# A 13-row store on one core, cut into blocks of 112, 12 and 4 partitions

## The chip, the cores and the metric

The kernel runs on one core of a Trainium2 chip. The metric is the device time of the whole program in microseconds (us). A core has five instruction streams: TensorE (PE), VectorE (DVE), ScalarE (ACT), GpSimd (POOL) and SyncE (SP). SP computes nothing; here it issues the transfers between the chip's main memory (DRAM) and the core's own memory, in which a tile has 128 partitions. The transfers are carried out by the core's 16 DMA engines.

## The reference

The input x has shape (1, 384, 384, 384) in bf16, channels last; w1d has a single element. Each channel's mean over all 384 x 384 positions is multiplied by that element, a sigmoid makes a scale per channel of it, and x is multiplied by the scale:

```python
g = jnp.einsum("bhwc->bc", x) / (H * W)
...
s = _sigmoid(g * w1d[0])     # k = 1, so there is no neighbour to add
return x * s[:, None, None, :]
```

(The third line is written out for k = 1.) The scale isn't known before all of x has been read, and x is 113 MB, more than the core's memory holds. A part of x has to be read twice.

## The kernel before

**Layout.** The 147456 positions are 1152 rows of 128 partitions; one row is 384 channels, 768 bytes in each partition. One tile named `arena` takes nearly the whole core memory and is addressed by rows. The input is cut into two chunks. `STREAMED` are rows that are read in the first pass, summed and dropped, and read again in the second pass. `KEPT` are rows that stay in the core between the passes. In each chunk partition p holds a contiguous stretch of DRAM, so that a transfer of n rows is 128 pieces of n x 768 contiguous bytes, one per partition.

**First pass.** Loads (`load`, line 235) bring rows in; TensorE sums them into PSUM (`sum_rows`, line 246). Many of the kept rows are packed so that four rows take three (`fold`, on VectorE and ScalarE); others are kept raw. At the end ScalarE computes the sigmoid (line 433) and copies it to PSUM (line 437).

**Second pass.** VectorE and GpSimd multiply rows by the scale (`scale`, line 446), packed rows are first unfolded (`unfold`, lines 280 and 286), and `store` (line 465) writes rows to the output. Rows that have been stored come free, and further rows of `STREAMED` are loaded into them, multiplied and stored. The raw kept rows go first, in ten pieces from `landed` (line 650 on) and three more that GpSimd multiplies (`alongside`); the last of the ten is `(A, 13)`, the 13 rows from row `A` of the arena on. Their place inside `KEPT` is `raw(A)`.

**Order.** All large transfers are issued by SP, in the order in which a planner (the loop from line 719 on) writes them out. The planner simulates time in steps of 0.05 us with costs per row and per transfer, and decides when a store or a load joins the list. The first load of the second pass is allowed only once all raw pieces have been sent. `Flow` (line 21) records every step and derives the waits: a step that overwrites arena rows waits for each step that reads them, and the transfers of one engine go round 24 semaphores (`LANES`), so that one of them also waits for the one 24 places earlier.

For the profile, the end of the first pass is at 267 us. After that SP issues 14 stores from 268.34 us on, with the changed one the last of them, at 280.67. Then follow three loads: 21 rows at 281.18, 13 rows, and at 287.77 13 rows into the place of the rows that the changed store reads. The next stores come from 295.25 on.

Of the kernel before, what the change touches and what calls it, by code (L numbers as in the profile page):

```python
# [131 lines left out]
def kernel(  # L132
# [11 lines left out]
    nc = tc.nc  # L144
    P = nc.NUM_PARTITIONS
# [18 lines left out]
    A = V + PAIR  # L164
# [27 lines left out]
    arena = pool.tile([P, ROWS, C], bf16, name="arena")  # L192
# [11 lines left out]
    of = out.rearrange("b h w c -> (b h w) c")  # L204

    def view(t, r0, n):
        return t[r0 * P : (r0 + n) * P, :].rearrange("(p r) c -> p r c", r=n)

    def rows(lo, n):
        return [("a", r) for r in range(lo, lo + n)]  # L210

    fl = Flow(nc, tc)
# [5 lines left out]
    STREAMED, KEPT = (0, N_STREAM + 1), (N_STREAM + 1, N_KEPT - 1)  # L218
# [9 lines left out]
    def raw(a):  # L228

        return c_raw + 1 + (a - U if a < G0 else PAIR + a - V)  # L230
# [65 lines left out]
    def fold(k):  # L296
# [46 lines left out]
        reads=["ones", "w_bf"], writes=["bank0"],  # L343
# [4 lines left out]
        reads=["bank0"], writes=["w_sc"],  # L348
# [38 lines left out]
    for i, bk in enumerate(banks):  # L387
        lo, hi = i * BANK, min((i + 1) * BANK, PS * C)
# [36 lines left out]
    for a, n in [(U, 8), (A, 20), (A + 20, 11), (A + 31, 8), (V, 8), (Y + 1, 6), (T + 5, 4), (T + 2, 3), (T, 2)]:  # L425
# [8 lines left out]
        reads=["bank0", "w_sc"], writes=["s_bf"],  # L434
# [6 lines left out]
    def scale(a, n, eng="DVE", s=s_bf, after=()):  # L441
        v = arena[:, a : a + n, :]
        vec = nc.vector if eng == "DVE" else nc.gpsimd
        fl.add(
            eng,
            lambda: vec.tensor_tensor(  # L446
                out=v, in0=v, in1=s[:, None, :].to_broadcast([P, n, C]), op=Op.mult
            ),
            reads=rows(a, n) + ["s_bf" if s is s_bf else "bank0"], writes=rows(a, n), after=after,
        )  # L450
# [6 lines left out]
    def scale_both(a, n):  # L457
# [4 lines left out]
        if m:  # L462
            scale(a + n - m, m, "POOL", after=before)

    def store(chunk, a, lo, hi):
        r0, n = chunk
        return fl.add(
            "SP",
            lambda: nc.sync.dma_start(out=view(of, r0, n)[:, lo:hi, :], in_=arena[:, a : a + hi - lo, :]),  # L469
            reads=rows(a, hi - lo), dma=True,  # L470
        )

    def unfold(g, first):

# [244 lines left out]
    while True:  # L719
# [12 lines left out]
        if dve_at <= now:  # L732
# [4 lines left out]
            if landed and (ahead < PENDING or not can):  # L737
                chunk, a, lo, n, end = landed.popleft()
# [18 lines left out]
        if alongside and alongside[0][0] <= now:  # L757
            _, chunk, a, lo, n = alongside.popleft()
            store(chunk, a, lo, lo + n)
            moves.append([now + LAT, n * ROW + PER_STORE, stored(a, n)])  # L760
        while waiting and waiting[0][0] <= now:
            _, n, then, chunk, a, lo, known = waiting.popleft()
            known.append(store(chunk, a, lo, lo + n))
            last_is_load = False
            sent_off += 1
            moves.append([now + LAT, n * ROW + PER_STORE, then])
# [10 lines left out]
        if bank_at is None and len(line) <= total - BANKS_AT and got and max(got)[0] > PS * 4 // 3:  # L777
            a = max(got)[1]
# [3 lines left out]
            for i, bk in enumerate(banks):  # L782
                lo, hi = i * BANK, min((i + 1) * BANK, PS * C)
# [6 lines left out]
        if got and todo < N_STREAM:  # L790
            n, a = max(got)
            n = min(n, CAP, N_STREAM - todo)
# [62 lines left out]
```

## Time and profile before

| | |
|---|---|
| median of three runs | 719.0 us (718.45 to 719.02) |
| the profiled execution | 718.35 us, its span 716.0 us |
| moved by DMA | 303.68 MB, 424 GB/s over the span |
| read from and written to DRAM | 190.32 MB and 113.25 MB |
| large transfers issued by SP | 110 |
| mean granted TensorE clock | 0.668 |

The span goes from the first to the last instruction; what lies around it belongs to the time but not to the profile. The profile lists busy time by engine, the chain of waits that ended last, and transfers with their size in KB (1024 bytes) and the time from issue to landing. A window is a stretch of the span with the busy time of every engine, the share of the 16 DMA engines that was busy, and GB/s; a packet (one contiguous piece of a transfer) is counted in the window in which it starts, so that short windows are coarse.

### The profile page before, as it was taken

How to read it: one execution, taken by the hardware profiler on the slowest of the kernel's cores; microseconds unless marked ns; L12 is line 12 of the kernel's file. 1: busy time of each engine (PE TensorE's matmuls, PEld its weight loads, DVE VectorE, ACT ScalarE, POOL GpSimd, SP SyncE). 2: the span in 40 equal slices, each digit the busy share in tenths (PEclk: the TensorE clock that was granted, in tenths of full speed). 3: DMA queues.
4: the chain of work that ended last, by engine and by line, in shares of the span. 5: the costliest groups of instructions: out<-in, count | busy, mean ns of one | idle time of the engine just before them, and what ended most of it. 6: DMA issues, size and time to landing. Idle time of an engine off the chain costs nothing.

```text
span 716.0 us, 2027 instructions
## 1 busy us (share of the span) xinstructions
PE 211.7 (30%) x1202; PEld 0.3 (0%) x3; DVE 467.5 (65%) x383; ACT 116.5 (16%) x97; POOL 98.1 (14%) x46
## 2 busy tenths in 40 slices
PE   4667967999598680000000000000000000000000
PEld 0000000000000000000000000000000000000000
DVE  4600001799989849999999999999940597006840
ACT  3700001476667630000110000000000000000000
POOL 0000000000000005414233431167100000000000
PEclk9899998999899995555555555555555555555555
DMA  9999999999999989999999999999999999999997
GB/s 375 434 446 419 439 431 425 452 417 434 427 430 426 429 349 384 412 414 435 425 430 436 441 425 436 457 421 421 455 409 458 426 425 445 430 428 436 442 438 308
DMA packets 15852, 303.68 MB, mean 424 GB/s; under 512 B 1762, under 2 KB 2274, under 8 KB 4962
## 3 DMA queue, kind: packets, MB, share of 16 engines
q1 hardware_dynamic: 15840, 303.57, 99.0%
q8 instruction: 4, 0.07, 0.0%
q14 instruction: 6, 0.05, 0.0%
q10 hardware_dynamic: 2, 0.00, 0.0%
HBM read 190.32 MB, written 113.25 MB: 424 GB/s over the span
## 4 chain that ended last, share of the span: by engine, by line
DMA 48%; DVE 29%; PE 16%; ACT 1%; issue 1%; DVEq 0%; another core or an unknown queue 0%; SPq 0%; POOLq 0%
DMA arena<-in_x_dram 37%; DVE arena L446 20%; PE bank L246 16%; DMA out_dram<-arena 12%; DVE arena L280 5%; DVE arena L286 4%; ACT arena L317 1%; DVEq L107 0%; SPq L240 0%; SPq L469 0%; ACT s_bf L433 0%; SPq L113 0%; SPq L850 0%; POOLq L107 0%
## 5 line engine op out<-in xcount | busy, mean ns | idle before, releaser
L246 PE MATMUL bank<-arena,ones 128*128 128x384 bf16 x1151 | 203.6, 341 | 46.6 <-DMA arena<-in_x_dram 46.6
L280 DVE TENSOR_SCALAR arena<-arena 128x1536 uint16<-128x1536 uint16 (+2 forms) x199 | 140.4, 750 | 105.2 <-DMA arena<-in_x_dram 98.3
L446 POOL TENSOR_TENSOR arena<-arena,s_bf 128x768 bf16<-128x768 bf16 (+3 forms) x42 | 97.9, 2334 | 426.8 <-ACT bank L437 267.9
L446 DVE TENSOR_TENSOR arena<-arena,bank 128x3072 bf16<-128x3072 bf16 (+13 forms) x61 | 138.0, 2303 | 4.8 <-DMA arena<-in_x_dram 4.1
L446 DVE TENSOR_TENSOR arena<-arena,s_bf 128x5376 bf16<-128x5376 bf16 (+4 forms) x27 | 76.5, 2901 | 94.9 <-DMA arena<-in_x_dram 84.8
L286 DVE TENSOR_TENSOR arena<-arena 128x3072 uint16<-128x3072 uint16 (+2 forms) x90 | 117.6, 1307 | 13.9 <-PE bank L246 11.1
L317 ACT ACTIVATE arena<-arena 128x3072 uint16<-128x3072 uint16 (+1 forms) x38 | 102.4, 2696 | 146.0 <-DVE arena L280 146.0
L556 PE MATMUL bank<-odd,ones 128*128 128x1 bf16 x1 | 0.2, 187 | 260.0 <-DVE odd L551 260.0
L384 ACT COPY arena<-bank 128x512 uint32<-128x512 uint32 (+2 forms) x8 | 4.2, 534 | 88.0 <-DMA out_dram<-arena 87.8
L246 PE MATMUL bank<-s_bf,ones 128*128 128x384 bf16 x48 | 8.3, 326 | 0.0
L317 ACT ACTIVATION_READ_ACCUMULATOR arena<-arena 128x1 f32 x38 | 7.1, 186 | 0.0
L384 ACT COPY bank<-arena 128x512 uint32<-128x512 uint32 (+2 forms) x8 | 3.8, 529 | 0.0
L260 PE MATMUL bank<-arena,ones 128*128 128x384 bf16 x1 | 0.5, 477 | 7.0 <-DMA arena<-in_x_dram 7.0
L433 ACT ACTIVATE s_bf<-bank,w_sc 128x384 bf16<-128x384 f32 x1 | 0.6, 581 | 9.4 <-PE bank L246 9.4
L823 ACT ACT_TABLE_LOAD x1 | 1.3, 1283 | 0.7 <-PEq L839 0.7
L337 DVE MEMSET ones<- 128x128 bf16 x1 | 0.2, 165 | 1.0 <-PEq L839 1.0
L342 PE MATMUL bank<-w_bf,ones 1*128 1x1 bf16 x1 | 0.2, 178 | 2.1 <-DMA w_bf<-in_w1d_dram 2.1
L347 DVE TENSOR_SCALAR w_sc<-bank 128x1 f32<-128x1 f32 x1 | 0.2, 158 | 0.9 <-PE bank L342 0.9
L560 DVE CAST odd_i<-bank 128x1 int32<-128x1 f32 x1 | 0.2, 157 | 0.3 <-PE bank L556 0.3
L437 ACT COPY bank<-s_bf 128x192 uint32<-128x192 uint32 x1 | 0.3, 323 | 0.0
L556 PEld LDWEIGHTS bank<-odd,ones 128*128 128x128 bf16 x1 | 0.1, 105 | 517.9 <-DVE odd L551 517.9
L384 ACT COPY arena<-rest 128x64 uint32<-128x64 uint32 x1 | 0.2, 246 | 0.0
(10 smaller groups left out, 1.4 us busy)
## 6 DMA issues: line engine op xcount, KB each, us to landing
arena<-in_x_dram SPq DMA_DIRECT2D x3, 6912.0 KB, 36.2
out_dram<-arena SPq DMA_DIRECT2D x3, 6912.0 KB, 28.4
arena<-in_x_dram SPq DMA_DIRECT2D x4, 4608.0 KB, 24.2
arena<-in_x_dram SPq DMA_DIRECT2D x6, 3072.0 KB, 19.4
out_dram<-arena SPq DMA_DIRECT2D x6, 3072.0 KB, 21.5
arena<-in_x_dram SPq DMA_DIRECT2D x2, 6144.0 KB, 31.4
arena<-in_x_dram SPq DMA_DIRECT2D x2, 4992.0 KB, 23.1
arena<-in_x_dram SPq DMA_DIRECT2D x1, 8160.0 KB, 26.4
```

What stands on the lines that cost most here:

```text
L246: return pe.add_instruction(mybir.InstMatmult(name=nc.get_next_instruction_name(), ins=[pe.lower_ap(rhs), pe.lower_ap(ones[:])], outs=[pe. ...
L260: return nc.tensor.matmul(acc, lhsT=ones[:], rhs=arena[:, i, :], start=first, stop=last)
L280: lambda: nc.vector.tensor_scalar(out=dst, in0=src, scalar1=s0, scalar2=s1, op0=op0, op1=op1),
L286: "DVE", lambda: nc.vector.tensor_tensor(out=dst, in0=a, in1=b, op=op), reads=reads, writes=writes
L317: lambda: nc.scalar.activation(out=y, in_=y, func=ACTF.Copy, accum_out=seen[:, 2 * k + i : 2 * k + i + 1]),
L337: fl.add("DVE", lambda: nc.vector.memset(ones[:], 1.0), writes=["ones"])
L384: "ACT", lambda: nc.scalar.copy(dst.bitcast(u32), src.bitcast(u32)), reads=reads, writes=writes
L433: lambda: nc.scalar.activation(out=s_bf[:], in_=acc, func=ACTF.Sigmoid, scale=w_sc[:, 0:1]),
L437: "ACT", lambda: nc.scalar.copy(s_ps.bitcast(u32), s_bf[:].bitcast(u32)), reads=["s_bf"], writes=["bank0"]
L446: lambda: vec.tensor_tensor(out=v, in0=v, in1=s[:, None, :].to_broadcast([P, n, C]), op=Op.mult),
L556: lambda: nc.tensor.matmul(votes, lhsT=ones[:], rhs=odd[:], start=True, stop=True),
L823: nc.scalar.preload_act_table(ACTF.Sigmoid)
```

## The change

The store whose chunk is `KEPT` and whose first row is `raw(A)`, the 13 rows from arena row `A`, is issued as three transfers, of partitions 0 to 111, 112 to 123 and 124 to 127. All other stores are issued as before. The planner still counts one store, and `store` returns the last of the three steps. A step that later overwrites these rows waits for all three.

```diff
+    STEPPED = raw(A)
+    BLOCKS = (0, 112, 124, P)
+
     def store(chunk, a, lo, hi):
         r0, n = chunk
-        return fl.add(
-            "SP",
-            lambda: nc.sync.dma_start(out=view(of, r0, n)[:, lo:hi, :], in_=arena[:, a : a + hi - lo, :]),
-            reads=rows(a, hi - lo), dma=True,
-        )
+        cuts = BLOCKS if (chunk, lo) == (KEPT, STEPPED) else (0, P)
+        for p, e in zip(cuts, cuts[1:]):
+            step = fl.add(
+                "SP",
+                lambda p=p, e=e: nc.sync.dma_start(
+                    out=view(of, r0, n)[p:e, lo:hi, :], in_=arena[p:e, a : a + hi - lo, :]
+                ),
+                reads=rows(a, hi - lo), dma=True,
+            )
+        return step
```

## Prediction

> **What bounds the kernel now.** I read the page first, for the part that is full, and then the windows of busy time by stretch, which carry bytes per second.
>
> ```profile
> span 716.0 us, 2027 instructions
> PE 211.7 (30%) x1202; PEld 0.3 (0%) x3; DVE 467.5 (65%) x383; ACT 116.5 (16%) x97; POOL 98.1 (14%) x46
> ...
> DMA  9999999999999989999999999999999999999997
> ...
> q1 hardware_dynamic: 15840, 303.57, 99.0%
> ```
>
> No compute engine is busy for two thirds of the span, while the 16 DMA engines are 99.0% busy on the one queue that SP issues. The time is set by bytes over DMA rate, and by whatever makes a DMA engine move bytes below its rate. So I looked for stretches in which the queue is full and the rate sags. The last two columns are the DMA share and GB/s.
>
> ```profile
> core 0: us, PE busy (x) PEld busy (x) DVE busy (x) ACT busy (x) POOL busy (x), PEclk, DMA share, GB/s
> 266.50:269.00 2.50, 0.80 (x5) 0.00 (x0) 1.05 (x3) 0.90 (x2) 0.65 (x1) 1.00 0.00 0
> ...
> 271.00:277.00 6.00, 0.00 (x0) 0.00 (x0) 6.00 (x4) 0.00 (x0) 6.00 (x3) 0.50 1.04 419
> 277.00:281.00 4.00, 0.00 (x0) 0.00 (x0) 4.00 (x4) 0.00 (x0) 0.56 (x1) 0.50 1.02 426
> ...
> 285.00:288.00 3.00, 0.00 (x0) 0.00 (x0) 2.90 (x4) 0.00 (x0) 0.00 (x0) 0.50 1.04 319
> 288.00:296.00 8.00, 0.00 (x0) 0.00 (x0) 6.79 (x4) 0.00 (x0) 2.38 (x2) 0.50 0.98 417
> 296.00:299.00 3.00, 0.00 (x0) 0.00 (x0) 3.00 (x2) 0.00 (x0) 2.53 (x2) 0.50 1.01 395
> 299.00:314.00 15.00, 0.00 (x0) 0.00 (x0) 14.86 (x10) 0.00 (x0) 4.74 (x2) 0.50 1.02 433
> 314.00:318.00 4.00, 0.00 (x0) 0.00 (x0) 3.93 (x3) 0.00 (x0) 0.00 (x0) 0.50 0.96 349
> ...
> 330.00:708.00 378.00, 0.19 (x1) 0.10 (x1) 268.77 (x154) 4.41 (x9) 71.17 (x31) 0.50 1.01 434
> ```
>
> From 330 to 708 us the rate is 434 GB/s without a break, across many switches between loads and stores. Between 285 and 318 us it sags three times although the engines count as busy (share 0.96 to 1.04), so packets take longer there; no engine lacks work. Against 434 the sags cost (434-319)x3/434 = 0.8 us, (434-395)x3/434 = 0.3 us and (434-349)x4/434 = 0.8 us, together 1.9 us for the mean DMA engine. The first sag begins where the store of the change meets the first load of the second pass:
>
> ```profile
> 280.67 0.33 SPq L469
> ...
> 281.18 12.22 DMA arena<-in_x_dram
> ```
>
> These are two pieces of the chain of waits: the store issued at 280.67 and the load at 281.18. The DMA view gives the time from issue to landing: of the 13-row store before it, of the changed store, and of the first and the third load of the second pass:
>
> ```profile
> out_dram<-arena SPq DMA_DIRECT2D x1, 1248.0 KB, 4.9
> ...
> out_dram<-arena SPq DMA_DIRECT2D x1, 1248.0 KB, 7.1
> ...
> arena<-in_x_dram SPq DMA_DIRECT2D x1, 2016.0 KB, 12.2
> ...
> arena<-in_x_dram SPq DMA_DIRECT2D x1, 1248.0 KB, 12.6
> ```
>
> The changed store lands at 280.67 + 7.1 = 287.8, having waited for what was queued ahead. The other end of the program shows how the DMA engines stand to each other (the last three stores on the timeline, the last one's time to landing, then the windows):
>
> ```profile
> 664.64 24.36 SPq L469 DMA_DIRECT2D out_dram<-arena  x3
> ...
> out_dram<-arena SPq DMA_DIRECT2D x1, 6816.0 KB, 25.9
> ...
> 709.40:710.60 1.20, 0.00 (x0) 0.00 (x0) 0.00 (x0) 0.00 (x0) 0.00 (x0) 0.50 0.94 409
> 710.60:711.50 0.90, 0.00 (x0) 0.00 (x0) 0.00 (x0) 0.00 (x0) 0.00 (x0) 0.50 0.01 0
> 711.50:712.60 1.10, 0.00 (x0) 0.00 (x0) 0.00 (x0) 0.00 (x0) 0.00 (x0) 0.50 0.35 149
> ```
>
> The last issue ends at 664.64 + 24.36 = 689.0 and takes 0.33, so it began near 688.66. A window counts a packet where it starts. The last store is 71 rows, so a packet is 71 x 768 = 54.5 KB: 149 x 1.1 = 164 KB are three packets. Three engines thus begin their last packet after 711.5, when all others have begun theirs before 710.6. The three run 0.9 us behind at the least; between the middles of the two groups (710.0 and 712.05) it is 2.0 us, which I take. The span ends with those three: the other thirteen have about 2.0 us of slack.
>
> **The change, part by part.** The bytes stay. One row of the store is 13 x 384 x 2 B = 9984 B per partition; an engine moves 426/16 = 26.6 GB/s (277 to 281 us), so a packet of one partition takes 0.375 us, and the whole store 8 packets per engine, 3.0 us.
>
> The 112 block is 7 packets for each of 16 engines. The 12 block can be at most one packet on 12 engines and the 4 block one packet on 4, if a partition is not cut. If both start from the same engine, four engines carry 9, eight carry 8 and four carry 7. The engines then reach the load up to two packets apart, 0.75 us. [...] No run here shows the assignment yet.
>
> Price of the extra packet: +0.375 us for the engines with 9, nothing for those with 8, -0.375 for those with 7. This is the lower bound, since a packet cannot beat its engine. The upper bound: the full store moves all 128 partitions in 3.0 us, so if it is the partitions (or what stands in front of a few of them) that limit and not the engines, a block takes 3.0 us however narrow; an engine with both small blocks then spends 7 x 0.375 + 3.0 + 3.0 = 8.6 us in place of 3.0, +5.6. I take the lower end, +0.4, for the forecast, since the tail's packets go with a single engine's rate: three alone show no other pace than all (a 54.5 KB packet at 26.6 GB/s is 2.05 us, and 712.6 + 2.05 = 714.65 is just the landing of the last store, 688.66 + 25.9 = 714.56). Those are big packets of whole stores, so I keep both ends for the range.
>
> [...]
>
> Issue: two more DMAs on SP at the 0.33 us of the row above put the first load from 281.18 to about 281.85. The cover is the stores queued ahead, which keep the engines busy until the changed store lands at 287.8, so it costs nothing; uncovered it would be 0.7 us. Completion of two more transfers: 271 to 277 us, with stores of 3 to 7 rows, runs at 419 against 434, 0.2 us in 6 us over some seven transfers: 0.03 each, 0.06 in all.
>
> The wait that follows: the third transfer of the second pass overwrites these 13 rows, so it now waits for three stores, and its SP instruction holds back what is queued behind.
>
> ```profile
> 281.18 6.91 SPq L240 DMA_DIRECT2D arena<-in_x_dram  x3
> ...
> 293.42 12.21 DVE L446 TENSOR_TENSOR arena<-arena,bank 128x3072 bf16<-128x3072 bf16 x5 [1.21 <-DMA arena<-in_x_dram]
> ...
> 295.25 8.54 SPq L469 DMA_DIRECT2D out_dram<-arena  x4
> ```
>
> Behind it stand the stores from 295.25, which wait for VectorE's multiplies of the first load, landed at 293.4. At 287.8 the two loads ahead still hold 3264 KB, 7.7 us of work; the wait can come 5 us later before an engine runs dry. Cost nothing, up to +5 us of lateness. The semaphore lanes shift by two, but the transfer 24 back is tens of microseconds old.
>
> What may go: the sags. After the first pass the DMA engines stand still (266.5 to 269 us, share 0.00) and start together, so 16 us later all switch from writing HBM to reading it in step, and the rate drops to 319. Once they have drifted apart, no switch sags. If the step keeps them from switching together, the first sag of 0.8 us goes for all, and the lag of the three, which can only have been made where engines are slowed unequally, is not built up, or less. The most to be had is 0.8 + 2.0 + 0.8 (the 314 sag) - 0.4 = 3.2 us, rounded up by the 296 sag to 3.5; the least that I call this case is 1.4. I take the three's 2.0, plus the first sag's 0.8, less 0.4 of extra packet, less 0.3 for what stays of the lag: -2.1 us. The profiled execution took 718.35 us, 2.35 around the span of 716.0; it becomes 716.25, with a span of 713.9. The median of the runs is 719.0, 0.65 above the profiled one, so 716.9.
>
> **Rivals.**
> *Nothing that a measurement of this kernel can tell (within 0.2%, 1.44 us).* The sags belong to what is read and written there, not to the step: then packets move by -0.4 to +0.4 us and the result is 718.6 to 719.4. For it: the sag at 314 to 318 comes 45 us after the common start, when engines are no longer together. Against it: no sag after 330 with the same kinds of switches. Here too belongs a first sag that goes alone, 0.8 - 0.4 = 0.4 us faster with the lag kept.
>
> *Slower: the narrow blocks crawl.* Place: the 12 and the 4 block. Price: between +0.4 and +5.6 us on the engines that carry both; the middle is 3.0. It decides where those engines have no cover: in the thirteen, 2.0 us is hidden, and it takes over 2.0 + 1.44 = 3.4 us to be slower by 0.2%; if they are among the three, or become late ones for which the later sags work as for the three now, 1.44 us does. [...] For it: late engines seem to be the ones that grow later. Against it: the packets of the three at the end keep the pace of one engine.
>
> *That the split doesn't happen* I give nothing: the condition asks for the chunk and the row of the 13 at A, which alone begin there, and each tail piece is sent by itself.
>
> **How the numbers follow.** Engines out of step, sags and lag mostly gone: 0.46, 715.3 to 717.56 us, likeliest 716.9; its own range with a weaker effect 715.3 to 717.9. No difference that can be told: 0.23, about 719. Slower by the narrow blocks: 0.31, 720.44 to over 722. The range that leaves out 2 in 10 runs from 715.3 (719.0 - 3.5, rounded) to 721.6, and loses the far end of the slow case (about 0.13) and a little below.
>
> **What would show it.** Right: the windows 285 to 288 and 314 to 318 above 380 GB/s in place of 319 and 349, and at the end no gap in packet starts as that from 710.6 to 711.5. Slower: the last of the three small stores lands over 3 us after the 112 block, and more than three packets start late at the end. No difference: the windows within 20 GB/s of before and three late packets. Wrong altogether if the span changes while the GB/s from 285 to 318 and the tail do not, or if SP or VectorE, not DMA, begins to hold the queue dry after 288 us.

## The result, and the profile after

The changed kernel is slower: 721.2 us against 719.0 us in the same session, ratio 1.0039 with a 95% interval of 1.0027 to 1.0052 (2.8 us, 1.9 to 3.7). Faster by 2.1 us was forecast; the value lies inside the stated range, on the other side of no change, and only because the range had been drawn wide enough for the slower rival. Where a ratio and a difference of medians disagree, here and below, the ratio with its interval is the one used.

The page after, its first lines and its DMA packets:

```profile
span 718.8 us, 2030 instructions
...
DMA packets 15868, 303.68 MB, mean 422 GB/s; under 512 B 1778, under 2 KB 2290, under 8 KB 4978
```

The bytes are the same. The page of before has 15852 packets, 1762 of them under 512 B. SP's queue had 15840 packets before, which are 110 large transfers with 128 + 16 each: one for each partition and 16 small ones, as many as there are DMA engines. I read the small ones as one for each engine that a transfer uses; the 16 new ones are then 12 + 4. The completion events in the trace of after agree: 16 for the 112 block, 12 for the 12 block and 4 for the 4 block, beside one at the issue of each of the small two. By this reading the small blocks used 12 and 4 engines; neither count tells which engines they are.

The windows of after at the stretches that the prediction read (last columns: DMA share and GB/s):

```profile
271.00:277.00 6.00, 0.00 (x0) 0.00 (x0) 6.00 (x4) 0.00 (x0) 6.00 (x3) 0.50 1.04 418
277.00:281.00 4.00, 0.00 (x0) 0.00 (x0) 4.00 (x4) 0.00 (x0) 0.63 (x1) 0.50 1.03 431
281.00:285.00 4.00, 0.00 (x0) 0.00 (x0) 3.93 (x4) 0.00 (x0) 0.00 (x0) 0.50 1.03 386
285.00:288.00 3.00, 0.00 (x0) 0.00 (x0) 2.93 (x3) 0.00 (x0) 0.00 (x0) 0.50 0.96 286
288.00:296.00 8.00, 0.00 (x0) 0.00 (x0) 4.25 (x3) 0.00 (x0) 0.00 (x0) 0.50 0.98 373
...
299.00:314.00 15.00, 0.00 (x0) 0.00 (x0) 14.93 (x9) 0.00 (x0) 6.93 (x4) 0.50 1.00 410
314.00:318.00 4.00, 0.00 (x0) 0.00 (x0) 3.90 (x4) 0.00 (x0) 0.00 (x0) 0.50 1.09 376
318.00:322.00 4.00, 0.00 (x0) 0.00 (x0) 3.96 (x3) 0.00 (x0) 0.00 (x0) 0.50 0.90 360
330.00:708.00 378.00, 0.19 (x1) 0.10 (x1) 271.11 (x155) 4.40 (x9) 72.79 (x32) 0.50 1.01 434
```

Up to 281 us and from 330 us on, the rates are those of before. In between lies most of the loss. One window over it, before and then after:

```profile
281.00:322.00 41.00, 0.00 (x0) 0.00 (x0) 39.41 (x24) 0.00 (x0) 11.64 (x6) 0.50 1.01 409
```

```profile
281.00:322.00 41.00, 0.00 (x0) 0.00 (x0) 36.82 (x23) 0.00 (x0) 9.65 (x5) 0.50 0.99 384
```

Against 434 GB/s that is (434 - 409) x 41/434 = 2.4 us lost before and (434 - 384) x 41/434 = 4.7 us after: 2.3 us more, of the 2.8 us by which the two spans differ. The rate falls by 6 per cent and the DMA share by 2 (1.01 to 0.99), so most of it is packets that take longer, and the smaller part engines without work. The chain of waits of after shows what else moved:

```profile
280.74 0.35 SPq L474
...
281.12 1.28 SPq L474
...
282.44 1.40 SPq L474
...
284.03 12.03 DMA arena<-in_x_dram
```

SP issues the 112 block in 0.35 us, the 12 block in 1.28 and the 4 block in 1.40, so that the first load is issued at 284.03 in place of 281.18. It lands at 296.06 in place of 293.40.

### The profile page after: what moved, and what is told of

It is laid out like the page before. It is cut to its first block, busy times and chain, and to the rows that moved or that the text cites. A ratio compares the mean times of both kernels' runs of the same rounds, so it can differ in the third digit from the quotient of the medians.

```text
span 718.8 us, 2030 instructions
## 1 busy us (share of the span) xinstructions
PE 213.1 (30%) x1202; PEld 0.3 (0%) x3; DVE 467.4 (65%) x383; ACT 116.5 (16%) x97; POOL 98.0 (14%) x46
## 4 chain that ended last, share of the span: by engine, by line
DMA 48%; DVE 29%; PE 16%; ACT 1%; SPq 1%; issue 1%; DVEq 0%; another core or an unknown queue 0%; POOLq 0%
DMA arena<-in_x_dram 37%; DVE arena L446 20%; PE bank L246 16%; DMA out_dram<-arena 11%; DVE arena L280 5%; DVE arena L286 4%; ACT arena L317 1%; SPq L474 0%; DVEq L107 0%; SPq L240 0%; ACT s_bf L433 0%; SPq L113 0%; SPq L858 0%; POOLq L107 0%
```

## The experiments

Three theories: **width** (transfers of fewer than 128 partitions move below the engines' rate), **step** (engines with 9, 8 and 7 packets reach the load unevenly), **queue** (SP's queue holds few transfers, so that two more of them delay the first load). Each kernel was timed beside the kernel before, in the same session. The edits below are abridged.

**At the place of the change.** The store cut by rows in place of partitions (rows3), the uncut store with a delayed first load (late), the cut made in an earlier store (earlier), and blocks of 112 and 16 (b112_16):

```diff
 rows3     BLOCKS = (0, 5, 9, 13), and out=view(of, r0, n)[:, lo + p : lo + e, :]
 earlier   STEPPED = raw(A + 13)
 b112_16   BLOCKS = (0, 112, P)
 late      store as before;
+          for i in range(22): hold = [fl.add("ACT", copy one column of a small tile, reads=rows(A, 1))]
-          load(STREAMED, a, todo, todo + n)
+          load(STREAMED, a, todo, todo + n, after=hold)      # first load of the second pass alone
```

> The 13-row store is cut by rows instead of partitions: 5, 4 and 4 rows of all 128 partitions. As many transfers as in the changed kernel, none narrow, all engines even. If SP's short queue is the cause (every transfer takes one of some four places, so the first load is queued later): the first load's issue ends near 285 us instead of 282.3 and the time is 720.5 to 721.5. If narrow blocks or the uneven engines are the cause: 719.0 within 0.7, and the first window (285 to 288) as before, near 319 GB/s.

> The uncut store of before; only the first load of the second pass waits some 4 us longer, for a chain of 22 tiny ScalarE copies. If the late first load is the cause: its issue ends near 285.5 as in the changed kernel, it lands near 296 and the time is about 721. If the blocks themselves cost: 719.0 within 0.7.

> The cut into 112, 12 and 4 partitions is made in the 13-row store three places earlier (rows A+13 to A+25), the last store is whole. Narrow blocks and uneven engines stay, but three whole stores stand between them and the first load, so that it is queued as in before (issue ends near 282.3). Short queue: 719.0 within 0.7. Narrow blocks or uneven engines: 720.5 or more, since engines stay uneven until the end.

> Blocks of 112 and 16 partitions: one transfer more than before, every engine has 7 + 1 packets. Short queue: the load is queued about half as late as in the changed kernel, 719.7 to 720.3. Uneven engines: 719.0. [...]

| kernel | ratio to before | 95% interval | us |
|---|---|---|---|
| rows3 | 1.0012 | 1.0001 to 1.0023 | +0.9 |
| late | 1.0009 | 0.9999 to 1.0019 | +0.6 |
| earlier | 1.0037 | 1.0024 to 1.0051 | +2.7 |
| b112_16 | 1.0022 | 1.0013 to 1.0031 | +1.6 |

(The us of this and the next tables are the ratio times the median of before.) The queue theory falls as the main cause. The delayed load was issued even later than in the changed kernel, landed at 293.58 us (before: 293.40), and cost 0.6 us at the most likely, with an interval that reaches no change:

```profile
281.49 4.88 ACT L810 COPY tick<-tick 128x1 f32<-128x1 f32 x22 [12.40 <-DVE arena L448]
286.40 1.75 SPq L241 DMA_DIRECT2D arena<-in_x_dram  x3
```

The earlier cut keeps the blocks and costs as much as the change. (Its first load came late as well, at 283.84, which I hadn't expected; the late run says that this is not what costs.) Its sag moved with the cut store, first the window of before, then that of the earlier cut:

```profile
277.00:285.00 8.00, 0.00 (x0) 0.00 (x0) 7.93 (x7) 0.00 (x0) 0.56 (x1) 0.50 1.03 430
285.00:296.00 11.00, 0.00 (x0) 0.00 (x0) 9.69 (x7) 0.00 (x0) 2.38 (x2) 0.50 1.00 390
```

```profile
277.00:285.00 8.00, 0.00 (x0) 0.00 (x0) 7.93 (x7) 0.00 (x0) 0.62 (x1) 0.50 0.97 332
285.00:296.00 11.00, 0.00 (x0) 0.00 (x0) 7.51 (x6) 0.00 (x0) 0.29 (x1) 0.50 0.99 384
```

From 277 to 285 us only stores are on the wire, and 332 against 430 GB/s is 1.8 us of DMA time. So the cut transfers are slow before any load comes. The second rows tell of the forecast's mechanism. I take a completion event in the trace, of which each of the 110 large transfers of before has 16, as one engine that has finished its share of a transfer; by these events the engines were already pulled apart (the 4-row store behind the cut completes on its 16 engines over 2.4 us, in the kernel before over 0.2), and still the stretch of the first load runs at 384 against 390. (The switch to loads came later there: 285 to 288 us alone rose from 319 to 394, and 288 to 296 fell from 417 to 380.) Being out of step did not remove the sag, though a part of this sag may be what the cut costs behind itself, as shown below.

**In a quiet stretch.** Two 13-row stores whose packets move from about 342 to 356 us, far from the first switch, were cut, and the store of the change left whole:

```diff
+    CUT, calls = (22, 25), [0]                       # which of the second pass's stores
-        cuts = BLOCKS if (chunk, lo) == (KEPT, STEPPED) else (0, P)
+        cuts = BLOCKS if calls[0] in CUT else (0, P)
 mid_12_4  (0, 112, 124, P)     mid_16  (0, 112, P)     mid_64  (0, 64, P)
 b64_64    the store of the change, cut (0, 64, P)
```

> The store in front of the first load is whole again. Two 13-row stores of the quiet stretch (issued near 330 and 342 us, on the wire near 341 to 356, where the rate was 430 to 455 GB/s) are cut into 112, 12 and 4 partitions instead. If such blocks crawl by themselves: each cut costs what it cost in the run with the earlier cut, about 1.5 to 2 us, the window 338 to 358 shows a sag, and the time is near 722. If the cost needs the common start or the first switch to loads: 718.2 to 719.4 and no sag.

> The same two stores cut into 112 and 16 partitions; every engine has 7 + 1 packets. If it is the uneven engines (9, 8, 7 packets): as before, 718.2 to 719. If it is transfers of fewer than 128 partitions: some 60 per cent of what the 112, 12, 4 cut costs in the same place, as it was in front of the load (0.22 against 0.39 per cent), about 720.5.

> The same two stores cut into two blocks of 64 partitions; every engine has 4 + 4 packets. If what limits a block is how many partitions (or what stands in front of them) it reaches: each block runs at half the rate, each store takes 6 us instead of 3, so +6 us for the two, 724 to 725. If only the engines limit: 718.2 to 719. If small blocks alone hurt: 719 to 720.

> The store in front of the first load cut into two blocks of 64 partitions; engines even, one transfer more. Reach of partitions: +3 us, 721 to 722. Uneven engines: as before. Short queue: at most +0.6, since the run with a late load showed a late load to cost nearly nothing.

Then a control by rows, the 112 block alone (partitions 112 to 127 of these rows are then not written), and either of the two stores alone:

```diff
 mid_rows    the two stores cut by rows, (0, 5, 9, 13)
 mid_112     (0, 112)
 mid_first   (0, 112, 124, P), CUT = (22,)
 mid_second  (0, 112, 124, P), CUT = (25,)
```

> The two 13-row stores of the quiet stretch are cut by rows, 5, 4 and 4 rows of all 128 partitions: as many transfers as with 112, 12 and 4, all of them full width. If it is transfers of fewer than 128 partitions that crawl: 718.2 to 719.3, no sag in 342 to 358. If more and smaller transfers (SP's queue, their completion) cost: 3 us or more, as the cut by partitions did.

> Only the 112 block of the two stores is issued; partitions 112 to 127 of those 26 rows are not written. That takes one packet of each engine away twice, -0.75 us in all if nothing else happens: 717.8. If the block of 112 crawls, though each of the 16 engines has 7 packets: most of the 6.9 us of the 112 and 16 cut stays, 721 to 724, and the difference to that run is the 16 block. If only narrow blocks crawl: 717.5 to 718.5.

> Only the first of the two stores is cut into 112, 12 and 4 partitions; the next 41 rows on the wire behind it are stores, then loads. If the price is in the blocks: half of the 6.0 us of the two, 721 to 722. If it takes a load behind the cut store: 718.5 to 719.5.

> Only the second of the two stores is cut; two loads come right behind it, as in the changed kernel. If the price is in the blocks: as the run with the first cut, 721 to 722. If the load behind it matters: all of the 6 us, about 724.

| kernel | ratio to before | 95% interval | us |
|---|---|---|---|
| mid_12_4 | 1.0083 | 1.0052 to 1.0114 | +6.0 |
| mid_16 | 1.0096 | 1.0065 to 1.0127 | +6.9 |
| mid_64 | 1.0070 | 1.0050 to 1.0090 | +5.0 |
| b64_64 | 1.0030 | 1.0020 to 1.0040 | +2.2 |
| mid_rows | 0.9996 | 0.9985 to 1.0006 | -0.3 |
| mid_112 | 1.0066 | 1.0042 to 1.0091 | +4.7 |
| mid_first | 1.0044 | 1.0029 to 1.0059 | +3.2 |
| mid_second | 1.0050 | 1.0030 to 1.0069 | +3.6 |

The window 342 to 362 us, in this order: before, mid_rows, mid_12_4, mid_16, mid_112, mid_64.

```profile
342.00:362.00 20.00, 0.00 (x0) 0.00 (x0) 19.72 (x13) 4.41 (x9) 4.30 (x3) 0.50 1.01 430
```

```profile
342.00:362.00 20.00, 0.00 (x0) 0.00 (x0) 19.54 (x12) 4.41 (x9) 5.30 (x2) 0.50 1.02 430
```

```profile
342.00:362.00 20.00, 0.00 (x0) 0.00 (x0) 17.02 (x10) 0.62 (x2) 3.10 (x1) 0.50 1.01 369
```

```profile
342.00:362.00 20.00, 0.00 (x0) 0.00 (x0) 16.91 (x10) 2.58 (x5) 3.10 (x1) 0.50 1.01 373
```

```profile
342.00:362.00 20.00, 0.00 (x0) 0.00 (x0) 18.65 (x12) 1.26 (x3) 3.27 (x2) 0.50 1.00 378
```

```profile
342.00:362.00 20.00, 0.00 (x0) 0.00 (x0) 17.33 (x11) 3.74 (x7) 3.10 (x1) 0.50 1.00 353
```

The engines are as busy as before (share 1.00 to 1.02), and the rate falls from 430 to between 353 and 378 GB/s. As many transfers at full width (mid_rows) cost nothing that can be measured: neither three transfers in place of one nor smaller packets are the trouble here. Blocks that leave all engines even (112 and 16; 64 and 64) cost as much as the uneven 112, 12, 4: the step theory falls. A load right behind the cut store makes no difference that these runs can tell (mid_first and mid_second overlap). What is left is width, and the surprise is the 112 block by itself. By the count it gives each of the 16 engines 7 packets, saves 0.75 us for the two stores, and yet costs 4.7. Of the fall in mid_12_4, (430 - 369) x 20/430 = 2.8 us lie in the window of the cut stores and their first followers; from 362 to 420 us that profile still runs below before:

```profile
362.00:420.00 58.00, 0.00 (x0) 0.00 (x0) 51.13 (x37) 3.79 (x8) 20.97 (x7) 0.50 1.00 412
```

Before has 435 there, so (435 - 412) x 58/435 = 3.1 us more go later, when every transfer that is issued has full width again. This does not follow every cut: mid_112 has the same 412 there, but mid_96 has 436 and mid_64 runs nearly as before:

```profile
362.00:420.00 58.00, 0.00 (x0) 0.00 (x0) 52.83 (x38) 0.67 (x3) 20.96 (x7) 0.50 1.01 432
```

**Which width, and how much of it at the place of the change.** Of the same two stores only partitions 0 to 95, 0 to 63 or 0 to 119 are issued; and in front of the first load only the 112 block.

```diff
 mid_96  (0, 96)    mid_lower  (0, 64)    mid_120  (0, 120)
 only_112   BLOCKS = (0, 112) in the changed kernel
```

> Of the two stores of the quiet stretch only partitions 0 to 95 are written: 6 packets on each of 16 engines, two fewer, so -1.5 us in all if nothing else happens (716.8). [...] If 7 packets per engine (an odd number) are the trouble: 716.5 to 717.5.

> Only partitions 0 to 63 are written: 4 packets per engine, four fewer, -3.0 us in all if nothing else happens (715.3). If two engines share what stands in front of their partitions, the half store takes as long as the whole one: 718 to 719, no gain at all. If it is the engines alone: 715 to 716.

> Only partitions 0 to 119 are written. 120 isn't a multiple of 16: if 15 engines take 8 packets each, one engine has none and nothing is gained or lost by the count (718.3). If widths below 128 are slow by themselves: 720 to 723, with the sag in 342 to 358.

> At the place of the change: only the 112 block of the store in front of the first load is issued, partitions 112 to 127 of its 13 rows are not written; one packet less per engine, -0.4 us, and no transfer more than before. If the 112 block carries most of the change's 2.8 us: 719.3 to 720.3 (before 718.3). If the 12 and 4 blocks do: 717.7 to 718.3.

| width | ratio to before | 95% interval | us | packets' time saved by the fullest engine | price of one store |
|---|---|---|---|---|---|
| 120 | 1.0051 | 1.0037 to 1.0066 | +3.7 | 0 | 1.8 |
| 112 | 1.0066 | 1.0042 to 1.0091 | +4.7 | 0.75 | 2.7 |
| 96 | 1.0042 | 1.0021 to 1.0063 | +3.0 | 1.5 | 2.3 |
| 64 | 0.9998 | 0.9985 to 1.0011 | -0.1 | 3.0 | 1.4 |
| only_112, in front of the load | 1.0010 | 0.9998 to 1.0023 | +0.7 | 0.4 | 1.1 |

(The time saved is 0.375 us for each packet that the fullest engine no longer has, for both stores. The price is the us and the time saved, halved for the two stores; an interval of 0.2 per cent is 1.5 us, so 1.8 to 2.7 are not told apart.) None of these widths is clean, and 7 packets have nothing to do with it: 6 and 8 packets cost as much within the intervals. Storing half the partitions takes as long as storing all (-0.1 us, with 3.0 us of packets saved). The page of mid_120 has 1760 packets under 512 B, two fewer than before; at one small packet for each engine, each of its 120-partition stores used 15 engines.

## Why the prediction was wrong, point by point

Two terms of the forecast's sum failed: the gain of 2.5 us (2.0 + 0.8 - 0.3) did not come, and the cost, taken at 0.4 us, was 2.8 if the gain was nothing. Together they make the 4.9 us between -2.1 and +2.8.

**The bound and the sags: right as read.** The time is DMA time, and 2.3 of the 2.8 us are a lower rate in 281 to 322 us.

**"The 112 block is 7 packets for each of 16 engines", priced at nothing: the first step that failed.** I counted packets per engine and took an engine's rate as given for any width. The price was looked for in the 12 and 4 blocks only. In the quiet stretch the 112 block alone costs 2.7 us a store, of the 3.0 to 3.6 that a cut into 112, 12 and 4 costs there. In front of the load it is smaller: 1.1 us for the 112 block (interval 0.2 to 2.0), 1.6 above before with 16 beside it, 2.8 as 112, 12 and 4. Why the same cut is cheaper there isn't settled; the stretch was already sagging, and slow packets may overlap with slow packets.

**Price of the 12 and 4 blocks: +0.4 taken, from bounds of 0.4 to 5.6.** Whether the lower end was right stays open. In front of the load 112, 12 and 4 cost 1.2 us more than 112 and 16, but the intervals overlap (1.9 to 3.7 and 0.9 to 2.2), and in the quiet stretch they cost 0.9 us less for two stores, within the intervals too. The argument for the lower end, that three late packets at the end keep one engine's pace, spoke of full-width stores and could not show a narrow one. The half store fits the premise of the upper end, that the partitions limit and not the engines: mid_lower takes as long as the full width (-0.1 us where 3.0 were saved). But by that premise the 112 block would have taken as long as the whole store, no longer, and it cost 4.7 us for the two. Why these widths are slow was not shown; no view here tells which engine serves which partition.

**The gain, sags and lag gone because engines are out of step: the second step that failed.** The rate over 281 to 322 us fell from 409 to 384 GB/s in place of rising, and the earlier cut, whose engines reach the load apart, sagged as before. In the quiet stretch, too, the 112 block pulled the engines apart (the second of its two stores completes over 5.7 us, that store in the kernel before over 2.7), and what followed ran at 412 against 435. The lag stayed as well: of the last store's packets three (109 x 1.5 = 164 KB) start late, as three did after 711.5 us before.

```profile
714.00:715.50 1.50, 0.00 (x0) 0.00 (x0) 0.00 (x0) 0.00 (x0) 0.00 (x0) 0.50 0.25 109
```

The forecast rested on two things that happened together (a common start at 268 us and the sags), with no row that tied one to the other. What makes the sags of the kernel before is still open.

**Issue and queue: half right.** Two issues were taken at 0.33 us each; they took 1.28 and 1.40. In the kernel before, the two loads issued next took 1.1 and 1.2 us by the trace, each with four transfers outstanding (issued and not yet landed). What SP waits for there is open: at 342.59 us four were outstanding as well, and the issue took 0.33. That the lateness is covered was right (late: +0.6, and no effect within its interval); rows3, which has late loads too, cost 0.9 (0.1 to 1.7), a part of which may be theirs.

**The slower rival** had the sign, and the measured 721.2 lies in its 720.44 to over 722. The upper end of the stated range, 721.6, stands 2.6 us above 719.0. No run shows such a term for the engines with both small blocks: the runs in front of the load cost 1.6 us with 112 and 16 and 2.8 with 112, 12 and 4, with overlapping intervals. The rival's place was too narrow: it put the price on the four engines with both small blocks, while the 112 block, with no small one behind it, is slow as well. By the completion events of the first load behind the cut, the first engine ends 0.8 us later than before and the last 2.7; the slowing is uneven there, and no view tells which engines it hits. By the last store all are late, the first by 2.6 us and the last by 2.8. So the cover of 2.0 us, which the other thirteen engines were said to have, hid nothing. Its tests did not come true: the last small store lands 0.8 us after the 112 block by the completion events, not over 3, and no more than three packets start late at the end.

## What to carry to other kernels

In a kernel bound by DMA as this one is, cut a store by its rows and keep all 128 partitions: three full-width pieces cost nothing that could be measured in the quiet stretch and 0.9 us (0.1 to 1.7) in front of the first load, while each cut of a store into blocks of partitions cost 1.6 to 3.6 us for a store that takes 3.0. (Only stores of 13 rows were cut; loads were not tried.) An even count of packets per engine wasn't an even or a full rate here (mid_112: 7 each, 378 against 430 GB/s); before pricing a new transfer shape from the packets of another shape, put one such transfer in a quiet stretch and look at the GB/s. When a rate sags and something else happens at the same time, look for a row in which only one of the two occurs before building a gain on it.

## What was not expected of the hardware

Two stores of 64 partitions took as long as two of 128 (-0.1 us), and a block that by the count gives every engine 7 packets slowed them all the same (mid_112: +4.7 us for two), and by unequal amounts (the second completes over 5.7 us, before over 2.7). A slow transfer went on costing after its last packet: in mid_12_4 about as much was lost from 362 to 420 us, behind the cuts, as in their window (3.1 and 2.8 us). It did hardly or not in mid_64 and mid_96 (432 and 436 against 435 GB/s), and why isn't known. And SP took 1.3 to 1.4 us to issue a transfer of 117 or 39 KB right behind another, about as long as it took in the kernel before for loads of 2016 and 1248 KB (1.1 and 1.2).
